# Nystrom attention with a sticky expert, one core: batch 0's queries and keys in single pairs, landmark sums on GpSimd, fewer first w1 transfers

## The chip, the core and the metric

The kernel runs on one core of a Trainium2 chip. Its engines work side by side and wait for each other through semaphores: TensorE (PE) multiplies into PSUM, VectorE (DVE) and ScalarE (ACT) work on PSUM and SBUF, GpSimd (POOL) on SBUF, and SyncE (SP) issues nearly all transfers (DMA). The metric is the device time of one execution in microseconds (us). Before the change the median of three runs is 450.06 us, from 449.97 to 450.13.

## The reference

Inputs are q, k and v of 8 batches with 8 heads, 576 tokens and 64 features, and the weights of 8 experts (w1 512 x 1024, w2 1024 x 512). First comes attention through 32 landmarks per head, each the mean of 18 neighbouring tokens:

```
q_lm = q.reshape(B, H, m, S // m, D).mean(axis=3)      # m = 32
k_lm = k.reshape(B, H, m, S // m, D).mean(axis=3)
A, Bm, C = sm(q, k_lm), sm(q_lm, k_lm), sm(q_lm, k)    # scaled softmax
Z = Bm.T / (norm1(Bm) * norminf(Bm) + 1e-06)
for _ in range(6):
    Z = 2 * Z - Z @ Bm @ Z
attn_out = A @ Z @ C @ v
```

Its output is the input of a mixture of experts: every token has the logits of 8 experts, takes the best one or keeps the expert of the token before it (by a local gate), and its output is `p[e] * (max(x @ w1[e], 0) @ w2[e])`.

## The kernel before

The batches go one after the other. Of each batch the attention part gives the factor `at` (A, transposed) and a small matrix `wt` (Z C v); x is never formed, since w1 is multiplied by `wt` into `g` (`w_w1`, L1236, for some 128-column blocks of w1 at a time, and `first_w1`, L1251, for block 0, whose slices of all 8 experts are loaded ahead). `split_g` (L1260) makes a high part `gh` on ScalarE and a low part `gl` on VectorE. `mm1` (L1286) then makes the hidden rows of block f out of six products (`gh` with two parts of `at`, and `gl` with one, for each of two head groups), and `expert` (L1313) the outputs with w2. One expert, chosen by a vote of the batch's tokens, serves a whole batch; the tokens of other experts are gathered at the end.

The order on each engine is the order in which this Python code emits instructions. Later batches' attention steps are spread between the expert's products by a table of times; `clock` and `at_time(t, ...)` put a step at a place and not at a time on the chip. Batch 0 has nothing to hide behind: `startup` (L933) is written out by hand. The names in it:

- `load` (L227) issues q and k of a batch. Heads lie in pairs (128 partitions hold two heads of 64 features), and a transfer moves one or two of four pairs. Every transfer has one of eight semaphores in turn, so a transfer waits until the one eight places before it has landed.
- `landmarks` (L254) sums 18 tokens to a landmark on VectorE, with GpSimd's help from batch 1 on; `landmark_scale` (L271) scales on ScalarE. For keys it writes the 32 landmarks behind the keys, so that a score product of 288 + 32 columns has those of the landmarks too.
- `score_c(g, hf, bank)` (L959) is C's scores of head group g, half hf of the tokens; `score_a` (L968) A's. `max_c`, `max_b`, `max_both` (L976 to L985) take maxima on VectorE, `max_b` with an exponential on ScalarE behind it; `exp_c` is C's exponentials; `turn_a` transposes A's scores.
- `lq0`, `lk0`, `lq2`, `lk2` are batch 1's landmarks in parts. `vote` (L859) leaves the expert's number in `regs`; SyncE and TensorE read it into a register, and the expert's weights are loaded (`load_w1` L1229, `load_w2` L1271).
- `keep_busy` (L926) and the loops at L189, L191 and L1174 are products whose result nobody reads.
- `second_block` (L1197) emits batch 1's scores C (`c_products`, L613), of which `c_max` (L624) takes maxima, together with blocks 1 to 3 of the first expert's w1.

Of the kernel before, what the change touches and what calls it, by code (L numbers as in the profile page):

```python
# [13 lines left out]
F32 = mybir.dt.float32  # L14
# [5 lines left out]
AX = mybir.AxisListType  # L20
# [4 lines left out]
P = 128  # L25
B, H, S, D = 8, 8, 576, 64
M = 32
# [36 lines left out]
def nystrom_attn_then_sticky_moe(ctx, tc, qT, kT, v, wg, w12, out):  # L64
# [121 lines left out]
        nc.vector.memset(ecs[g][:, S:], 0.0)  # L186
    nc.vector.memset(v_t[64:128, 4 * DM:], 0.0)
    pz = one.tile([P, 512])
    for _ in range(11):  # L189
        nc.tensor.matmul(pz, zeros[:, 0:P], zeros, start=True, stop=True)  # L190
    for _ in range(18):  # L191
        nc.tensor.matmul(pz[:, 0:16], zeros[:, 0:P], zeros[:, 0:16], start=True, stop=True)


    events, clock, serial = [], [0.0], itertools.count()
# [20 lines left out]
    def at_once(parts):  # L216
        for _ in parts:
            pass
# [8 lines left out]
    def load(b, st):  # L227
        for t in "qk":
            load_qk(b, st, t, b % 2)
        q, k = ("q", qT, S), ("k", kT, S)  # L230
        pieces = [(x, slice(a, a + 2)) for a in (0, 2) for x in (q, k)]
        if b == 0:
            pieces[2:] = [(x, slice(a, a + 1)) for x in (q, k) for a in (2, 3)]
        for (t, src, n), a in pieces:
            nc.sync.dma_start(out=st[t][:, a, 0:n], in_=src[b][:, a])
        if b == 0:
            nc.sync.dma_start(out=wg_sb[0:D], in_=wg)
# [16 lines left out]
    def landmarks(b, st, t, a):  # L254


        src = st[t][:, :, 0:S].rearrange("p a (l t) -> p a l t", t=SEG)
        s = sm.tile([P, 2, M], F32, name="s" + t)
        if b == 0:
            for i in (0, 1) if a else (slice(0, 2),):  # L260
                nc.vector.reduce_sum(out=s[:, i], in_=src[:, a + i] if a else src[:, i], axis=AX.X)  # L261
        else:
            t9 = at.tile([P, 2, M, 9], F32, name="t9")
            for i in range(2):
                nc.gpsimd.tensor_add(t9[:, i], src[:, a + i, :, 0:9], src[:, a + i, :, 9:18])  # L265
            yield 1
            nc.vector.reduce_sum(out=s, in_=t9, axis=AX.X)  # L267
            yield 0.75
        landmark_scale(st, t, a, s)

    def landmark_scale(st, t, a, s):  # L271
# [338 lines left out]
    def c_begin_rest(st, banks):  # L610
        st["pc"][1].extend(x.tile([P, 512])[:, 0:96] for x in banks)

    def c_products(st, k0, n):  # L613


        out, x = (st["pc"][1], 0) if k0 == 512 else (st["pc"][0], k0)
        for c in range(4):
            for g in range(2):
                h = head(g, c)
                r = slice(64 * (h % 2), 64 * (h % 2) + 64)  # L620
                nc.tensor.matmul(out[g][32 * c:32 * c + 32, x:x + n], st["ql"][r, h // 2, :],
                                 st["k"][r, h // 2, k0:k0 + n], start=True, stop=True)
# [310 lines left out]
    def startup(st, nx):  # L933
# [34 lines left out]
        def score_a(g, hf, bank):  # L968
            pa[g, hf] = bank[0].tile([P, 512], F32, name=bank[1])
            for c in range(4):  # L970
                h = head(g, c)
                r = slice(64 * (h % 2), 64 * (h % 2) + 64)
                nc.tensor.matmul(pa[g, hf][32 * c:32 * c + 32, 0:288], st["k"][r, h // 2, S:S + M],
                                 st["q"][r, h // 2, 288 * hf:288 * hf + 288], start=True, stop=True)

        def max_c(g, hf):  # L976
            nc.vector.reduce_max(out=nm[g][:, hf:hf + 1], in_=pc[g, hf][:, 0:288], axis=AX.X, negate=True)
# [14 lines left out]
        def turn_a(g, hf):  # L992
            nc.vector.transpose(out=sa[:, g, 9 * hf:9 * hf + 9, :].rearrange("p j l -> p (j l)"), in_=pa[g, hf][:, 0:288])

        at_once(landmarks(0, st, "q", 0))
        score_c(0, 0, (psa, "one"))
        at_once(landmarks(0, st, "k", 0))
        score_c(0, 1, (psa, "one"))
        score_a(0, 0, (py, "py"))
        score_a(0, 1, (pg, "pg"))  # L1000
        max_c(0, 0)
        at_once(landmarks(0, st, "q", 2))
        score_c(1, 0, (psa, "one"))
        at_once(landmarks(0, st, "k", 2))
        score_c(1, 1, (py, "py"))
        max_c(0, 1)
        max_b(0)
        max_both(0)
        turn_a(0, 0)
        max_b(1)  # L1010
        exp_c(0)
# [159 lines left out]
        vote(st, lq0)  # L1171
        keep_busy(3)
        pz = one.tile([P, 512])
        for _ in range(22):  # L1174
            nc.tensor.matmul(pz[:, 0:16], ones, ones[:, 0:16], start=True, stop=True)

        e = st["e"] = expert_of(regs[0:1, 0:1], (ET.SP, ET.PE))
        st["w1", 0] = load_w1(e, 0, ((nc.sync, 1, 1, 0, P), (nc.sync, 2, 1, 0, P), (nc.sync, 3, 1, 0, P)))
        get_w2(0, 0)
        get_w2(0, 1)  # L1180
        st["w1", 1] = load_w1(e, 1, ((nc.sync, 0, 2, 0, P), (nc.sync, 2, 2, 0, P)))
        get_w2(0, 2)
        get_w2(0, 3)
        mine = sm.tile([P, 1], F32, name="mine0", bufs=1)
# [12 lines left out]
        def second_block():  # L1197
            c_begin(nx, (one, one))
            c_begin_rest(nx, (one, Banks((pg, "pg"))))
            c_products(nx, 0, 512)  # L1200
            lk2(0)
            lk2(1)
            g1 = w_w1(st, 0, 1, 1, ((py, "py"), (py, "py")))
            next(g1)
            c_products(nx, 512, 96)
            c_max(nx, 1, (0,))
            at_once(g1)

        at_time(0.02, second_block)
        at_time(0.6, c_max, nx, 1, (1,))  # L1210
        at_time(1.005, lambda: at_once(w_w1(st, 0, 2, 2, ((py, "py"), (py, "py")))))
        at_time(1.3, c_max, nx, 0)
        at_time(1.31, c_exp_b, nx)
        at_time(1.52, c_bound, nx)
# [625 lines left out]
```

## Time and profile before

| | |
|---|---|
| median of 3 runs | 450.06 us (449.97 to 450.13) |
| profiled execution | 451.21 us, its span on the core 449.4 us |
| TensorE busy | 435.1 us (97%), 4898 products |
| VectorE busy | 284.5 us (63%) |
| ScalarE busy | 216.0 us (48%) |
| GpSimd busy | 192.0 us (43%) |
| chain that ended last | PE 77%, DVE 13%, ACT 5%, issue 2%, DMA 1%, POOL 1% |

Times in rows count from the span's start. Busy time is what instructions of an engine cover; the times of products are modelled ends of a pipelined engine. The chain is followed back from the last instruction, at each step to what released it. A share of the whole span says little about a stage: the first 41 us, which the change touches, have their own limits.

### The profile page before, as it was taken

To read this page: it belongs to the slowest core of one execution; us is meant where nothing else is said; L and a number is where in the kernel's file an instruction comes from. 1 tells how busy PE (TensorE), PEld (TensorE's weight loads), DVE (VectorE), ACT (ScalarE), POOL (GpSimd) and SP (SyncE) were. 2 spreads that over 40 slices of the span, in tenths; PEclk is the share of its full clock that TensorE was granted. 3 is DMA by queue.
4 is the path that set the end of the run, shared out by engine and by line. 5 is a ranking of instruction groups with operands and counts; after the bars stand their busy time and mean duration, and the time that the engine had idled before them with its cause. 6 is when DMAs were issued, how large, how long until landed. Compare 5 with 4: busy or idle time off the path is not lost.

```text
span 449.4 us, 12512 instructions
## 1 busy us (share of the span) xinstructions
PE 435.1 (97%) x4898; PEld 337.1 (75%) x4898; DVE 284.5 (63%) x869; ACT 216.0 (48%) x577; POOL 192.0 (43%) x235
## 2 busy tenths in 40 slices
PE   8888999999999999999999999999999999999996
PEld 3455777777786788878887788788887778776885
DVE  7878786666858576665766574656555786954111
ACT  2546525467354751566253752465145414445611
POOL 5456663165815664263632650174116601055520
PEclk9999999999999999999999999999999999999999
DMA  8959952779569697649957615831164315692211
GB/s 303 378 198 350 367 190 98 268 287 261 210 160 382 202 388 159 245 164 341 290 138 260 237 54 125 318 110 48 55 233 158 113 44 173 252 313 95 97 31 50
DMA packets 62365, 91.53 MB, mean 204 GB/s; under 512 B 26731, under 2 KB 28267, under 8 KB 61152
## 3 DMA queue, kind: packets, MB, share of 16 engines
q1 hardware_dynamic: 60960, 86.23, 57.0%
q0 software_dynamic: 1344, 4.48, 2.7%
q8 instruction: 39, 0.64, 0.6%
q14 instruction: 22, 0.18, 0.1%
HBM read 75.27 MB, written 15.47 MB: 202 GB/s over the span
## 4 chain that ended last, share of the span: by engine, by line
PE 77%; DVE 13%; ACT 5%; issue 2%; DMA 1%; POOL 1%; SPq 0%; DVEq 0%; ACTq 0%; POOLq 0%
PE py L1337 33%; PE ph L1295 19%; PE pg L1346 5%; PE ph L1247 2%; PE one L416 2%; PE one L463 1%; DVE h L1307 1%; PE one L562 1%; PE py L1573 1%; DMA k_t<-kT 1%; PE one L517 1%; DVE gl L1269 1%; PE one L825 1%; POOL t L265 1%; DVE sk L261 1%
## 5 line engine op out<-in xcount | busy, mean ns | idle before, releaser
L1337 PE MATMUL py<-wh,h 128*128 128x512 f32 x504 | 161.6, 403 | 0.1
L1284 POOL TENSOR_TENSOR wl<-raw,wh 128x512 fp32r<-128x512 f32 x64 | 82.2, 1293 | 70.8 <-ACT wh L1282 69.7
L1302 ACT ACTIVATE h<-ph 128x256 fp32r<-128x256 f32 (+1 forms) x128 | 52.4, 413 | 111.2 <-PE ph L1295 94.2
L1337 PEld LDWEIGHTS py<-wh,h 128*128 128x128 f32 x504 | 86.4, 189 | 25.2 <-issue 13.2
L1307 DVE SCALAR_TENSOR_TENSOR h<-ph,h 128x256 fp32r<-128x256 f32 x128 | 53.0, 416 | 61.0 <-ACT h L1302 58.2
L1337 PE MATMUL py<-wl,h 128*128 128x512 f32 x252 | 80.5, 400 | 0.0
L1295 PE MATMUL ph<-ath,gh 128*128 128x320 f32 (+1 forms) x256 | 77.5, 303 | 1.5 <-ACT gh L1266 0.8
L1295 PE MATMUL ph<-ath,gl 128*128 128x320 f32 (+1 forms) x256 | 75.8, 296 | 0.0
L1295 PE MATMUL ph<-atl,gh 128*128 128x320 f32 (+1 forms) x256 | 75.6, 295 | 0.0
L1295 PEld LDWEIGHTS ph<-ath,gh 128*128 128x128 f32 x256 | 48.4, 189 | 9.1 <-ACT h L1302 2.2
L1337 PEld LDWEIGHTS py<-wl,h 128*128 128x128 f32 x252 | 45.9, 188 | 11.6 <-issue 1.3
L1295 PEld LDWEIGHTS ph<-atl,gh 128*128 128x128 f32 x256 | 48.3, 189 | 3.9
L1295 PEld LDWEIGHTS ph<-ath,gl 128*128 128x128 f32 x256 | 48.3, 189 | 0.2 <-DVE gl L1269 0.2
L1282 ACT CAST wh<-raw 128x512 fp32r<-128x512 f32 x69 | 43.2, 627 | 2.2 <-DMA raw<-w 1.4
L1406 POOL TENSOR_TENSOR ys<-ys,yl 64x512 f32<-64x512 f32 x8 | 10.3, 1281 | 58.5 <-ACT yl L1404 58.5
L265 POOL TENSOR_TENSOR t<-q_t 128x288 f32<-128x288 f32 x20 | 14.5, 747 | 23.5 <-DVE sk L267 23.5
L423 DVE TENSOR_TENSOR et<-et,one 128x64 f32<-128x64 f32 x36 | 7.9, 220 | 24.7 <-ACT et L422 16.4
L794 POOL TENSOR_TENSOR sa<-sa,rsa 128x1152 f32<-128x1152 f32 x7 | 14.9, 2133 | 19.9 <-DVE s L693 13.2
L265 POOL TENSOR_TENSOR t<-k_t 128x288 f32<-128x288 f32 x22 | 17.0, 795 | 11.9 <-DVE sq L267 10.8
L1346 PE MATMUL pg<-wl,h 128*128 128x512 f32 x56 | 21.9, 391 | 0.0
L1346 PE MATMUL pg<-wh,h 128*128 128x512 f32 x56 | 21.8, 390 | 0.0
L1395 ACT ACTIVATE ys<-py,token 128x512 f32<-128x512 f32 x30 | 19.0, 685 | 5.0 <-PE py L1337 4.7
(435 smaller groups left out, 729.3 us busy)
## 6 DMA issues: line engine op xcount, KB each, us to landing
raw<-w SPq DMA_DIRECT2D x75, 256.0 KB
raw<-w SPq DMA_DIRECT2D x16, 1024.0 KB
k_t<-kT SPq DMA_DIRECT2D x9, 1152.0 KB
q_t<-qT SPq DMA_DIRECT2D x9, 1152.0 KB
out<-ys SPq DMA_DIRECT2D x31, 256.0 KB
v_t<-v SPq DMA_DIRECT2D x20, 256.0 KB
ad<-sa POOLq DMA_DIRECT2D x7, 576.0 KB, 3.1
v_t<-v SPq DMA_DIRECT2D x3, 1024.0 KB
```

Source lines behind the costliest of these rows:

```text
L265: nc.gpsimd.tensor_add(t9[:, i], src[:, a + i, :, 0:9], src[:, a + i, :, 9:18])
L416: return {1: lambda: each_place(lambda g, r: nc.tensor.matmul(pn[r, g, :], et[r, g, 0:32], et[r, g, n0:64], start=True, stop=True))}, part ...
L794: nc.gpsimd.tensor_tensor(out=sa, in0=sa, in1=rs.unsqueeze(2).broadcast_to([P, 2 * NJ, M]), op=ALU.mult)
L1282: by(out=wh, in_=raw)
L1284: rest.tensor_tensor(out=wl, in0=raw, in1=wh.bitcast(F32), op=ALU.subtract)
L1295: mm = nc.tensor.matmul(hp, w[:, g, c], x[:, g, s0:s0 + n], start=(i == 0), stop=(i == 5))
L1302: nc.scalar.activation(out=h[:, 0:e], in_=hp[:, 0:e], func=AF.Relu)
L1307: nc.vector.scalar_tensor_tensor(out=h[:, 384:384 + m], in0=hp[:, 0:m], scalar=0.0, in1=h[:, 0:m].bitcast(F32), op0=ALU.max, op1=ALU.subtract)
L1337: nc.tensor.matmul(yps[k], h[:, part + i * P:part + i * P + P], w, start=(f == 0 and part == 0 and w is wh), stop=(f == NC2 - 1 and part = ...
L1346: nc.tensor.matmul(yps[4], hs[ff][1], w, start=(ff == 0 and w is w2[ff][0]), stop=(ff == NC2 - 1 and w is w2[ff][1]))
L1395: nc.scalar.mul(out=ys, in_=yp, mul=st["pw"][:, k:k + 1])
L1406: nc.gpsimd.tensor_tensor(out=ys[0:64], in0=ys[0:64], in1=yl[0:64], op=ALU.add)
```

## The change

In `load`, batch 0's q and k go in eight transfers of one pair each, queries 0 and 1, keys 0 and 1, queries 2 and 3, keys 2 and 3, instead of six. In `startup`, the sums of these landmarks are taken apart: pairs 0 and 1 and queries 2 and keys 3 on VectorE alone, queries 3 and keys 2 first in GpSimd (18 tokens added to 9) and then on VectorE (`landmark_sums`). The maxima of group 0 move ahead of the last landmark sums. The first weights are issued as two transfers (block 1, blocks 2 and 3) and one (second half), instead of three and two. In `second_block` half of the large score products, two of four places of both groups, moves behind the product with w1 block 1, and the score products of the last 64 tokens and the landmarks move behind those with blocks 2 and 3. The warm-up products before the start are 12 wide ones instead of 11 wide and 18 small ones, and 39 small ones instead of 22 stand before the first product with w1.

```diff
-    for _ in range(11):
+    for _ in range(12):
         nc.tensor.matmul(pz, zeros[:, 0:P], zeros, start=True, stop=True)
-    for _ in range(18):
-        nc.tensor.matmul(pz[:, 0:16], zeros[:, 0:P], zeros[:, 0:16], start=True, stop=True)
...
         if b == 0:
-            pieces[2:] = [(x, slice(a, a + 1)) for x in (q, k) for a in (2, 3)]
+            pieces = [(x, slice(a + i, a + i + 1)) for a in (0, 2) for x in (q, k) for i in (0, 1)]
...
-    def c_products(st, k0, n):
+    def c_products(st, k0, n, places=range(4)):
...
-        for c in range(4):
+        for c in places:
...
-        at_once(landmarks(0, st, "q", 0))
+        (_, q01), (_, k01), (q23_half, q23), (k23_half, k23) = [landmark_sums(st, t, a) for a in (0, 2) for t in "qk"]
+        q23_half(1)
+        k23_half(0)
+        q01(0, True)
+        q01(1, True)
         score_c(0, 0, (psa, "one"))
-        at_once(landmarks(0, st, "k", 0))
+        k01(0, True)
+        k01(1, True)
         score_c(0, 1, (psa, "one"))
         score_a(0, 0, (py, "py"))
         score_a(0, 1, (pg, "pg"))
+        q23(0, True)
         max_c(0, 0)
-        at_once(landmarks(0, st, "q", 2))
+        max_b(0)
+        max_c(0, 1)
+        max_both(0)
+        q23(1)
         score_c(1, 0, (psa, "one"))
-        at_once(landmarks(0, st, "k", 2))
+        k23(0)
+        k23(1, True)
         score_c(1, 1, (py, "py"))
-        max_c(0, 1)
-        max_b(0)
-        max_both(0)
         turn_a(0, 0)
...
-        for _ in range(22):
+        for _ in range(39):
             nc.tensor.matmul(pz[:, 0:16], ones, ones[:, 0:16], start=True, stop=True)
 
         e = st["e"] = expert_of(regs[0:1, 0:1], (ET.SP, ET.PE))
-        st["w1", 0] = load_w1(e, 0, ((nc.sync, 1, 1, 0, P), (nc.sync, 2, 1, 0, P), (nc.sync, 3, 1, 0, P)))
+        st["w1", 0] = load_w1(e, 0, ((nc.sync, 1, 1, 0, P), (nc.sync, 2, 2, 0, P)))
         get_w2(0, 0)
         get_w2(0, 1)
-        st["w1", 1] = load_w1(e, 1, ((nc.sync, 0, 2, 0, P), (nc.sync, 2, 2, 0, P)))
+        st["w1", 1] = load_w1(e, 1)
...
-            c_products(nx, 0, 512)
+            c_products(nx, 0, 512, (0, 1))
             lk2(0)
             lk2(1)
             g1 = w_w1(st, 0, 1, 1, ((py, "py"), (py, "py")))
             next(g1)
-            c_products(nx, 512, 96)
+            c_products(nx, 0, 512, (2, 3))
             c_max(nx, 1, (0,))
             at_once(g1)
...
         at_time(1.005, lambda: at_once(w_w1(st, 0, 2, 2, ((py, "py"), (py, "py")))))
+        at_time(1.007, c_products, nx, 512, 96)
         at_time(1.3, c_max, nx, 0)
```

The function that GpSimd's halves come from stood there before, for batch 1: `half(i)` adds 9 tokens to 9 on GpSimd, `part(i, alone)` sums 18 of the source (alone) or 9 of GpSimd's result on VectorE, and part 1 is followed by the scaling.

VectorE's instructions in the start, before, from the first landmark sum on (`DMAHW0` to `DMAHW7` are the eight semaphores of the transfers; `one`, `py` are PSUM banks):

```order
L261 TENSOR_REDUCE sq<-q_t_217 128x64 [waits DMAHW0_49]
L261 TENSOR_REDUCE sk<-k_t_218 128x64 [waits DMAHW1_49]
L977 TENSOR_REDUCE nm<-one 128x1 [waits PE_49]
L261 TENSOR_REDUCE sq<-q_t_217 128x32 [waits DMAHW2_49]
L261 TENSOR_REDUCE sq<-q_t_217 128x32 [waits DMAHW3_49]
L261 TENSOR_REDUCE sk<-k_t_218 128x32 [waits DMAHW4_49]
L261 TENSOR_REDUCE sk<-k_t_218 128x32 [waits DMAHW5_49]
L977 TENSOR_REDUCE nm<-one 128x1 [waits PE_49]
L980 TENSOR_REDUCE nm<-one 128x1
L985 TENSOR_TENSOR nm<-nm 128x1 [waits DVE_49]
L993 STREAM_TRANSPOSE sa<-py 128x288 [waits PE_49]
L980 TENSOR_REDUCE nm<-py 128x1 [waits PE_49]
```

The same engine and place after the change, from queries 2 on, behind the four single sums of pairs 0 and 1 (`h` holds GpSimd's halves; L971, L974, L979, L987 are the old L977, L980, L985, L993):

```order
L307 TENSOR_REDUCE sq<-q_t_200 128x32 [waits DMAHW4_49]
L971 TENSOR_REDUCE nm<-one 128x1 [waits PE_49]
L974 TENSOR_REDUCE nm<-one 128x1 [waits PE_49]
L971 TENSOR_REDUCE nm<-one 128x1 [waits Activation_49]
L979 TENSOR_TENSOR nm<-nm 128x1 [waits DVE_49]
L307 TENSOR_REDUCE sq<-h 128x32 [waits Pool_49]
L307 TENSOR_REDUCE sk<-h 128x32 [waits Pool_49]
L307 TENSOR_REDUCE sk<-k_t_201 128x32 [waits DMAHW7_49]
L987 STREAM_TRANSPOSE sa<-py 128x288 [waits PE_49]
L974 TENSOR_REDUCE nm<-py 128x1 [waits PE_49]
```

Two maxima and the minimum of group 0 now stand ahead of the last three landmark sums; the second of the wide maxima has a wait for ScalarE, and two sums wait for GpSimd.

GpSimd's instructions at this place after the change; before, the rows without L304 stood there alone:

```order
L113 IOTA t_94 128x64 [waits Pool_49]
L304 TENSOR_TENSOR h<-q_t_200 128x288 [waits DMAHW5_49]
L115 CAST eb<-t_94 128x128 [waits Pool_49]
L304 TENSOR_TENSOR h<-k_t_201 128x288 [waits DMAHW6_49]
L101 IOTA t_94 128x8 [waits Pool_49]
L103 CAST ranks<-t_94 128x8 [waits Pool_49]
```

The halves stand between constants, and a constant behind a half waits with it for the landing.

VectorE in the second block, before, from the low parts of w1 block 0 on:

```order
L1269 TENSOR_TENSOR gl<-py,gh 128x128 [waits Activation_49] x2
L313 TENSOR_REDUCE sk<-h 128x32 [waits Pool_49] x2
L631 TENSOR_REDUCE nm8c<-one 128x1 [waits PE_49]
L1269 TENSOR_TENSOR gl<-py,gh 128x128 [waits Activation_49] x2
L1307 SCALAR_TENSOR_TENSOR h<-ph,h 128x256
L1310 SCALAR_TENSOR_TENSOR atl<-ph,atl 128x64
L631 TENSOR_REDUCE nm8c<-one 128x1
```

TensorE in the second block, after, behind the products of hidden block 0 (L615 is `c_products`, the old L621; L1249 the product with w1, the old L1247; L1297 `mm1`, the old L1295):

```order
L615 MATMUL one<-k_t_214,ql 32x512 x4
L1249 MATMUL py<-raw_630,wt 32x128 x8
L615 MATMUL one<-k_t_214,ql 32x512 x4
L1297 MATMUL ph<-ath,gh 128x320
L1297 MATMUL ph<-atl,gh 128x320
L1297 MATMUL ph<-ath,gl 128x320
```

Before, all eight of the first row stood ahead of the product with w1, and the small score products behind it. VectorE's order is as before here, but its first maximum reads what the second part of the score products writes.

## Rows read from the trace of the kernel before

**Rows 1.** Stages: engine busy us (instructions), then PEclk, DMA share, GB/s.
```profile
6.00:12.00 6.00, 5.11 (x75) 1.86 (x73) 5.80 (x12) 1.39 (x7) 1.56 (x8) 1.00 1.05 371
12.00:28.30 16.30, 13.43 (x293) 7.25 (x290) 13.43 (x46) 8.91 (x28) 8.77 (x9) 1.00 0.86 316
28.30:41.00 12.70, 10.65 (x141) 6.84 (x138) 9.86 (x34) 6.64 (x30) 7.41 (x10) 1.00 0.83 269
41.00:449.40 408.40, 401.15 (x4390) 319.40 (x4386) 252.26 (x769) 197.42 (x511) 169.26 (x165) 1.00 0.58 194
```
**Rows 2.** Chain that ended last, first 14 us: start, length, what.
```profile
1.20 4.75 DMA k_t<-kT
...
10.84 0.79 PE py L965 x8
...
11.65 0.20 DVE nm L980
```
**Rows 3.** VectorE in order of time: start, us, engine, line, op, operands.
```profile
5.97 1.35 DVE L261 TENSOR_REDUCE sk<-k_t 128x64 f32<-128x1152 f32 x1
...
7.62 1.40 DVE L261 TENSOR_REDUCE sq<-q_t 128x32 f32<-128x576 f32 x2
8.99 1.50 DVE L261 TENSOR_REDUCE sk<-k_t 128x32 f32<-128x576 f32 x2
10.41 0.45 DVE L977 TENSOR_REDUCE nm<-one 128x1 f32<-128x288 f32 x1
...
12.29 0.17 DVE L176 TENSOR_SCALAR sums<-sums 128x2 f32<-128x2 f32 x1
```
**Rows 4.** SyncE's issues in order of time.
```profile
5.97 0.38 SPq L235 DMA_DIRECT2D q_t<-qT  x1
7.47 0.38 SPq L235 DMA_DIRECT2D k_t<-kT  x1
...
9.74 0.47 SPq L941 DMA_DIRECT2D wg_sb<-wg  x1
```
**Rows 5.** ScalarE behind the group 1 maximum.
```profile
11.88 0.29 ACT L981 ACTIVATE bm<-py,nm 128x32 f32<-128x32 f32 x1 [0.44 <-DVE nm L980]
```
**Rows 6.** A half on GpSimd, and the sum of one on VectorE, batch 1's.
```profile
20.99 0.74 POOL L310 TENSOR_TENSOR h<-q_t 128x288 f32<-128x288 f32 x1
...
23.74 0.41 DVE L313 TENSOR_REDUCE sk<-h 128x32 f32<-128x288 f32 x1
```
**Rows 7.** TensorE, its weight loads and VectorE in the second block.
```profile
28.38 0.70 PE L1175 MATMUL one<-ones 128*128 128x16 bf16 x22
31.46 1.09 PE L621 MATMUL one<-k_t,ql 64*32 64x512 f32 x16
32.39 0.18 PEld L1247 LDWEIGHTS py<-raw,wt 64*32 64x32 f32 x16 [0.75 <-DMA raw<-w]
32.39 0.45 PE L1247 MATMUL py<-raw,wt 64*32 64x128 f32 x16
32.64 0.69 DVE L631 TENSOR_REDUCE nm8c<-one 128x1 f32<-128x512 f32 x1 [0.86 <-PE one L621]
33.25 0.48 DVE L1269 TENSOR_TENSOR gl<-py,gh 128x128 fp32r<-128x128 f32 x2
```
**Rows 8.** GpSimd, VectorE and TensorE around TensorE's gap at 39 us.
```profile
36.89 0.61 POOL L1282 CAST wh<-raw 128x512 fp32r<-128x512 f32 x1 [0.49 <-DMA raw<-w]
37.58 1.29 POOL L1284 TENSOR_TENSOR wl<-raw,wh 128x512 fp32r<-128x512 f32 x1
37.59 1.34 DVE L849 SCALAR_TENSOR_TENSOR eq<-pe,keys 128x40 f32<-128x40 f32 x1
39.94 0.59 PE L1247 MATMUL ph<-raw,wt 64*32 64x512 f32 x1 [0.97 <-DVE atl L1310]
```
**Rows 9.** Wide products whose result nobody reads, early and late.
```profile
1.23 4.88 PE L190 MATMUL one<-sa 128*128 128x512 bf16 x11 [1.23 <-DVE sa L180]
...
26.59 1.04 PE L930 MATMUL one<-ones 128*128 128x512 bf16 x4
```

More of the change, by code (lines that the diff above doesn't have):

```diff
@@ L258, in landmarks @@
         s = sm.tile([P, 2, M], F32, name="s" + t)
[L259 to L268, printed above, removed]
+        t9 = at.tile([P, 2, M, 9], F32, name="t9")
+        for i in range(2):
+            nc.gpsimd.tensor_add(t9[:, i], src[:, a + i, :, 0:9], src[:, a + i, :, 9:18])
+        yield 1
+        nc.vector.reduce_sum(out=s, in_=t9, axis=AX.X)
+        yield 0.75
         landmark_scale(st, t, a, s)
```

## The prediction

> **What bounds the kernel now.** I read the busy times by stage first, then the chain of waits of the first 14 us, then VectorE, SyncE, ScalarE and GpSimd in order of time there, and last the stretch from 28 to 41 us. From 41 us to the end TensorE is busy 401.15 of 408.40 us [rows 1]: nothing that the change touches lies there, and a shift of what comes before is carried to the end one for one. From 6 to 12 us VectorE is the busy one, 5.80 of 6.00 us [rows 1]. The chain of that stretch [rows 2] goes from the landing of batch 0's first key pairs (1.20 + 4.75 = 5.95) through VectorE to the last score product on TensorE at 10.84 and a maximum on VectorE at 11.65. I take this last point, the group 1 maximum, as the measure of the start: from there on both kernels issue the same VectorE, ScalarE and TensorE instructions down to the vote, in the same order, each waiting for the one before. So whatever moves 11.65 moves the vote, the expert's first loads and the end.
>
> **The start, step by step.** Before, VectorE runs without a gap from 5.97 to 10.49: keys 0 and 1 (1.35), a maximum, queries 2 and 3 (1.40), keys 2 and 3 (1.50) [rows 3]. What is left (a maximum of 0.45 at 10.41, a small one, a minimum, a transpose) is done while ScalarE and TensorE turn the last landmarks into scores, from 10.49 to 11.65: 1.16 us of cover. The new order spends this cover earlier: only the transpose stays behind the last landmark sum, the rest goes ahead of it.
>
> When do the pairs land? SyncE shows it: its later transfers wait for a landing each, of keys 0 and 1 at 5.97, queries 2 at 7.47, keys 3 at 9.74 [rows 4]. The three pairs behind queries 2 take 2.27, some 0.75 each, which puts queries 3 at 8.23 and keys 2 at 8.98. The bytes ahead of key pair 1 stay the same, so I leave its landing at 5.97. Splitting gains this: pair 0 is summed before pair 1 lands, and after 5.97 one sum of half of 1.50 = 0.75 remains instead of 1.35: done at 6.72 instead of 7.32, 0.60 gained.
>
> From 6.72 VectorE does: queries 2, 0.70 (half of 1.40), to 7.42; the first maximum, 0.45, to 7.87; the group 0 maximum, whose scores are ready at 6.72 + 1.16 = 7.88, 0.20, to 8.08. Then the next maximum waits for ScalarE, by the order. In the trace the same pair of steps stands at 11.65: the maximum of 0.20 [rows 2] ends at 11.85, ScalarE's exponential starts at 11.88 [rows 5], and VectorE goes on behind it at 12.29 [rows 3]: 0.44 of standstill. So 8.52; a maximum of 0.45 and the minimum to 9.07; two sums of GpSimd's halves at 0.41 [rows 6], to 9.87; keys 3 alone, 0.75, to 10.6; and the 1.16 of ScalarE and TensorE behind it: 11.75. So 0.60 from the split and 0.58 from GpSimd's halves (two times 0.70 less 0.41) are eaten by the wait of 0.44 and by the maxima and the minimum, some 0.8, that lost their cover: **+0.1 us**.
>
> That is with landings by size. The trace has one that is not: 5.97 to 7.47 is 1.50 for one pair, twice 0.75, and all later ones keep that delay [rows 4]. Before, it cost nothing, VectorE was busy. After, queries 2 are wanted at 6.72. If they land at 7.47 again, VectorE stands 0.75; GpSimd starts queries 3 at 8.23 and, with 0.74 a half [rows 6] and a small cast that the order puts between its two halves, ends keys 2 at about 9.9; VectorE ends keys 3 at 11.35: 12.5, or **+0.85**. GpSimd is strictly in line: what waits behind its first half is that cast, the second half and two constants that are needed much later. As the trace is one execution and doesn't show the delay's cause, I take the middle of the ends, **+0.5**; the lower bound is -0.35, if the wait for ScalarE were hidden.
>
> [...]
>
> The warm-up ends with its twelfth wide product; the next product but one waits for ScalarE anyway: nothing. SyncE's eight issues are ahead of the data: nothing.
>
> **28 to 41 us.** (a) 39 instead of 22 small products: 22 take 0.70 [rows 7], so 17 more are at most 0.54, by the spacing rather 0.43, and the large scores, behind expert 0's first products, move from 31.46 to about 31.9. Half of them (of 1.09) ends at 32.45, and the first w1 slice is waited for until 32.39 [rows 7]: hidden, and if the slice lands earlier nothing is gained. (b) In the new order the other half, 0.55, stands behind that w1 product of 0.45, and VectorE's maximum over all of them ahead of the low halves "gl". Before, that maximum began at 32.64 and gl at 33.25 [rows 7]. Now the scores end at 33.4, the maximum (0.69) at 34.1, gl follows: 0.75 to 0.85 later, and TensorE's third product of that slice waits for it. So TensorE is late by 0.7. (c) Two w1 transfers and one for the second half, instead of three and two: each saves SyncE some 0.5, but the transfer engines are 83% busy in this stretch [rows 1]; the landing gains 0 to 0.35.
>
> Against this stands the gap of TensorE before 39.94, 0.97 us [rows 8]. What ends it is VectorE: the step at 37.59 lasts 1.34 while GpSimd's subtraction runs from 37.58 for 1.29 [rows 8]; the products free their bank only after that. A delay of 0.7 puts this step at about 38.3, still inside GpSimd's subtraction, whose cast waits for a weight landing and not for TensorE (0.49 before 36.89 [rows 8]). So the gap takes up the delay: 0, with bounds -0.35 (loads earlier) and +0.3 (if (a) and (b) add up beyond 0.97). I take **-0.05**.
>
> **Sum.** +0.5 - 0.05 = +0.45 on the profiled execution's 451.21 us (span 449.4, 1.8 around it); it is 1.15 above the median of the timed runs, and the same difference on 450.06 gives **450.5 us**. What a measurement of this kernel can tell from no change is about 0.2%, 0.9 us: 449.16 to 450.96.
>
> **Rivals.**
> 1. The loads come forward (faster). If splitting lets key pair 1 land one pair earlier (0.75), and the fewer w1 transfers free VectorE's step at 37.59 and the second half's product, it is -0.65 in the start and -0.35 to -0.9 later: about 449.0. For it: 4.75 us from issue to landing [rows 2], where four pairs at 0.75 need 3.0. Against it: the bytes ahead of key pair 1 are unchanged.
> 2. The landings decide (slower). Place: VectorE's wait for queries 2 and GpSimd's waits for queries 3 and keys 2. Where the delay of 0.75 returns and a second one falls on queries 3 or keys 2, nothing of it is covered any more; price 0.85 + 0.75 = 1.6: 451.6. It decides once keys 2 land after about 8.7 (0.74 later GpSimd ends when VectorE is ready, 9.07 + 0.41). For it: there is such a delay, in the one execution traced [rows 4]. Against: the three pairs behind it keep 0.75.
> [...]
> 4. GpSimd's halves save nothing, since VectorE waits for them: the upper end of the forecast, +0.85, 450.9.
>
> **Chances.** The forecast with its own range, 449.9 to 451.0: 0.55. Rival 1: 0.19. Rival 2: 0.16. Rival 3: 0.05. Rival 4 by itself: 0.05. The whole range, 449.0 to 451.4, leaves out rival 3 and the far ends of 1 and 2. Faster than 449.16: most of rival 1, 0.16. Slower than 450.96: rivals 2 and 3 and a small part of the forecast, 0.24. Within: 0.60.
>
> **What would show it.** The group 1 maximum between 11.6 and 12.5; VectorE idle for about 0.4 behind the group 0 maximum, waiting for ScalarE; key pair 1's landing at 5.9 to 6.0; VectorE waiting for queries 2 if SyncE's second batch 1 transfer starts at 7.4, and not if at 6.7; gl of the second w1 slice 0.7 later against the start of that slice, and the gap before the second half's w1 product smaller by as much. The prediction is wrong if that maximum comes before 11.2, if the ScalarE wait is missing, if the gap at 39 us stays beside the delayed gl, or if the granted clock falls.

## The result, and the profile after

The changed kernel takes 453.31 us (median of 5 runs, 452.73 to 455.02), the kernel before 450.06 (449.97 to 450.4): a ratio of 1.0079, 95% interval 1.0062 to 1.0095. It is slower by 3.25 us where 450.5 was forecast, outside the range of 449.0 to 451.4. The profiled execution took 454.88 us, its span 453.1. Executions of over 800 us, which a few kernels had, are left out of every ratio.

The first thing to see is in the page's slices, TensorE's busy tenths and its granted clock: a dent in the first two slices, and a lower clock in the third, which the kernel before does not have. Before, then after:

```profile
PE   8888999999999999999999999999999999999996
PEclk9999999999999999999999999999999999999999
```

```profile
PE   7689999999999999999999999999999999999996
PEclk9989999999999999999999999999999999999999
```

Then by stages (engine busy us, then PEclk, DMA share, GB/s), against the second row of [rows 1], where the clock is 1.00 from 12 to 28.3 us:

```profile
20.00:22.00 2.00, 1.14 (x50) 0.78 (x49) 1.94 (x6) 0.48 (x1) 2.00 (x3) 1.00 1.04 382
22.00:24.00 2.00, 0.92 (x30) 0.74 (x33) 0.51 (x3) 0.68 (x1) 2.00 (x3) 0.67 1.04 382
24.00:26.00 2.00, 2.00 (x43) 1.09 (x42) 1.55 (x5) 0.52 (x2) 0.10 (x2) 0.50 0.40 144
26.00:28.00 2.00, 1.79 (x23) 0.64 (x21) 1.10 (x3) 0.68 (x3) 1.77 (x2) 0.97 0.00 0
```

TensorE in order of time there (start, us, engine, line, op, operands; in brackets the idle time ahead and what ended it):

```profile
20.73 0.41 PE L667 MATMUL pg<-v_t,ect 128*32 128x64 f32 x10
23.09 0.86 PE L667 MATMUL pg<-v_t,ect 128*32 128x64 f32 x22 [1.95 <-issue]
...
25.05 1.32 PE L924 MATMUL ph<-ones 128*128 128x512 bf16 x3
```

In the middle of 32 equal products TensorE stands for 1.95 us and waits for nothing that the profile shows ("issue"). Behind it the granted clock is 0.50 until about 26: a wide product takes 0.44 (3 in 1.32) as in the warm-up of [rows 9], not 0.26. The chain that ended last holds this standstill as a piece of its own:

```profile
21.14 1.95 issue
25.11 1.26 PE ph L924 x3
```

The start was late too. VectorE, against [rows 3]:

```profile
6.10 1.64 DVE L307 TENSOR_REDUCE sk<-k_t 128x32 f32<-128x576 f32 x2 [0.89 <-DMA k_t<-kT]
7.83 0.75 DVE L307 TENSOR_REDUCE sq<-q_t 128x32 f32<-128x576 f32 x1
...
9.53 0.46 DVE L971 TENSOR_REDUCE nm<-one 128x1 f32<-128x288 f32 x1 [0.45 <-ACT bm L975]
...
10.96 0.74 DVE L307 TENSOR_REDUCE sk<-k_t 128x32 f32<-128x576 f32 x1
...
12.86 0.19 DVE L974 TENSOR_REDUCE nm<-py 128x1 f32<-128x32 f32 x1 [0.77 <-PE py L959]
```

The group 1 maximum is at 12.86 instead of 11.65. SyncE's issues show why, as in [rows 4] (each waits for a landing: 6.98 for key pair 1, 7.82 for queries 2, 9.37 for keys 2, 10.15 for keys 3):

```profile
6.98 0.36 SPq L233 DMA_DIRECT2D q_t<-qT  x1
7.82 0.38 SPq L233 DMA_DIRECT2D k_t<-kT  x1
...
9.37 0.38 SPq L233 DMA_DIRECT2D k_t<-kT  x1
10.15 0.47 SPq L935 DMA_DIRECT2D wg_sb<-wg  x1
```

Key pair 1 lands at 6.96, not at the 5.97 that I had kept.

The way of the lateness through the traces, from the starts of equal instructions in both: +1.21 at the group 1 maximum, +4.04 at expert 0's first product (33.35 instead of 29.31), +3.58 at the second half of its w1 (43.52 instead of 39.94), +4.0 behind 132 us, +5.0 behind 212, +3.65 at the last product. The drop at the end is an accident of the trace of before: there TensorE's products over the last expert's w1 took 1.3 longer, from 408.31 on, with a wait at 409.59. Of the other traces only the four at the end of the experiments (r1 to r4) have it, and by its size it makes up the difference between the 451.21 of that execution and the median of 450.06.

### The profile page after: what moved, and what is told of

Its sections match the earlier page's. It is cut to its first block, busy times and chain, and to the rows that moved or that the text cites. A ratio compares the mean times of both kernels' runs of the same rounds, so it can differ in the third digit from the quotient of the medians.

```text
span 453.1 us, 12512 instructions
## 1 busy us (share of the span) xinstructions
PE 436.3 (96%) x4898; PEld 338.0 (75%) x4898; DVE 283.6 (63%) x871; ACT 215.9 (48%) x577; POOL 193.3 (43%) x237
## 4 chain that ended last, share of the span: by engine, by line
PE 78%; DVE 12%; ACT 5%; issue 2%; DMA 1%; POOL 1%; SPq 0%; DVEq 0%; ACTq 0%; POOLq 0%
PE py L1339 33%; PE ph L1297 19%; PE pg L1348 5%; PE ph L1249 2%; PE one L410 2%; PE one L457 1%; PE one L556 1%; DVE h L1309 1%; PE py L1575 1%; DMA q_t<-qT 1%; PE one L511 1%; PE one L819 1%; POOL t L259 1%; PE ph L1554 1%; DVE gl L1271 1%
## 5 line engine op out<-in xcount | busy, mean ns | idle before, releaser
L1297 PE MATMUL ph<-ath,gh 128*128 128x320 f32 (+1 forms) x256 | 77.5, 303 | 1.1 <-ACT gh L1268 0.4
L1297 PE MATMUL ph<-ath,gl 128*128 128x320 f32 (+1 forms) x256 | 75.9, 296 | 0.4 <-DVE gl L1271 0.4
L1297 PE MATMUL ph<-atl,gh 128*128 128x320 f32 (+1 forms) x256 | 75.6, 295 | 0.0
L1297 PEld LDWEIGHTS ph<-ath,gh 128*128 128x128 f32 x256 | 48.4, 189 | 9.2 <-ACT h L1304 2.2
L1339 PEld LDWEIGHTS py<-wl,h 128*128 128x128 f32 x252 | 45.9, 188 | 11.6 <-issue 1.3
L1297 PEld LDWEIGHTS ph<-atl,gh 128*128 128x128 f32 x256 | 48.3, 189 | 3.9
L1297 PEld LDWEIGHTS ph<-ath,gl 128*128 128x128 f32 x256 | 48.3, 189 | 0.9 <-DVE gl L1271 0.8
L788 POOL TENSOR_TENSOR sa<-sa,rsa 128x1152 f32<-128x1152 f32 x7 | 15.0, 2137 | 20.7 <-DVE s L687 14.0
```

What stands on the lines that cost most here:

```text
L788: nc.gpsimd.tensor_tensor(out=sa, in0=sa, in1=rs.unsqueeze(2).broadcast_to([P, 2 * NJ, M]), op=ALU.mult)
L1297: mm = nc.tensor.matmul(hp, w[:, g, c], x[:, g, s0:s0 + n], start=(i == 0), stop=(i == 5))
L1339: nc.tensor.matmul(yps[k], h[:, part + i * P:part + i * P + P], w, start=(f == 0 and part == 0 and w is wh), stop=(f == NC2 - 1 and part = ...
```

## The experiments

The kernel before, run beside the others each time, had medians of 450.47 (e1 to e4), 450.23 (e5, e7 to e9), 450.50 (e10, e11) and 450.13 (e12, e13). A ratio is not the quotient of two medians and can differ from it by some 0.2%.

**Two theories.** Theory F: TensorE's instructions come in blocks, by transfers of their own. The traces of before and after hold 9921 of them: 4898 products, as many weight loads, and 125 that its sequencer runs (waits, registers). Counted all together, in order of time, four are places at which TensorE stands, in one trace or in several, without a releaser and goes on 1.2 to 1.5 us behind the end of a packet of one kind: the 450th, the 706th, the 3522nd and the 5570th, which are 256, 12 times 256 and 20 times 256 behind the first. (Without those of the sequencer the distances are not multiples of 256.) The packets are instructions, 39 of 16 KB on a queue of their own (the page; queue and kind: packets, MB, share), and 39 times 256 is 9984, about TensorE's 9921:

```profile
q8 instruction: 39, 0.64, 0.6%
```

Among the transfers of 20.5 to 20.6 us is the one that matters (packets, MB, share of that tenth of a microsecond):

```profile
q8 instruction: 1, 0.02, 68.5%
```

It takes 1.10 us from 20.53, and TensorE goes on 1.46 behind its end. I call the block from the 450th instruction on block 3, the one from the 706th block 4. In before, block 3's fetch begins at 15.49 and is ready 1.3 ahead of its need, if TensorE can go on 1.46 behind its end there too. The warm-up lost 18 small products and gained a wide one; with their weight loads that is 34 instructions less, so the edge behind which block 3 is asked for by this theory (the 194th) moved from 13.3 to 16.7 us. Theory L: the late landings, and what follows from them, are the whole cause.

**1. The pairs back (e1).** The changed kernel, with before's warm-up and small products.

```diff
-    for _ in range(12):
+    for _ in range(11):
         nc.tensor.matmul(pz, zeros[:, 0:P], zeros, ...)
+    for _ in range(18):
+        nc.tensor.matmul(pz[:, 0:16], zeros[:, 0:P], zeros[:, 0:16], ...)
...
-        for _ in range(39):
+        for _ in range(22):
```

> The changed kernel with the warm-up of before (11 wide and 18 small products) and 22 instead of 39 small products behind the vote. Theory F (instruction fetch): TensorE's instructions come in blocks of 256, and block 3 (from the 450th traced instruction on) arrived at 23.09 us because the 34 instructions that were removed ahead of it made its request come some 3 us later; the standstill of 1.95 us and the half clock of 22.9 to 26 us follow from that. With the instructions back, no gap over 0.3 us at the 450th instruction, granted clock 1.00 throughout, and what is left is the start's shift of 0.5 to 1.25: 450.3 to 451.3 us. Rival L (landings): the late landings of batch 0's pairs and what follows from them are the cause; the standstill stays and the time too: 452.7 to 453.5.

Measured: 451.19 us, 1.0021 (1.0009 to 1.0033). The same products run through, and the only wait left is one for VectorE that before has as well; TensorE:

```profile
20.22 0.65 PE L669 MATMUL pg<-v_t,ect 128*32 128x64 f32 x32
21.38 0.33 PE L1058 MATMUL ph<-yl 32*32 32x32 f32 x16 [0.51 <-DVE yl L1065]
```

**2. The pairs away, nothing else (e2).** The same edit the other way round, on the kernel before.

> The kernel before with the changed warm-up alone (12 wide products, no small ones) and 39 small products behind the vote; all else as before. F: the request of block 3 moves from 13.3 to about 15.5 us, the block is ready at 20.2 to 21.9 and wanted at 19.6: a gap of 0.6 to 2.3 us at the 450th instruction, and perhaps a lower clock behind it; 450.6 to 452.5 us. L: 449.9 to 450.3, no gap.

Measured: 451.96 us, 1.0039 (1.0024 to 1.0055), single times from 450.66 to 455.9, granted clocks from 1.00 down to 0.990. Its trace has the standstill, at the 450th instruction; TensorE:

```profile
19.98 0.41 PE L671 MATMUL pg<-v_t,ect 128*32 128x64 f32 x10
22.46 0.86 PE L671 MATMUL pg<-v_t,ect 128*32 128x64 f32 x22 [2.07 <-issue]
```

These two decide for F. About half of the loss, by e1 rather seven tenths, is made by a part of the change that computes nothing.

**3. The start alone (e3), the second block alone (e4).** e3 is e1 with the w1 transfers and large scores of before; e4 is the kernel before with those two changed.

```diff
-        st["w1", 0] = load_w1(e, 0, ((nc.sync, 1, 1, 0, P), (nc.sync, 2, 1, 0, P), (nc.sync, 3, 1, 0, P)))
+        st["w1", 0] = load_w1(e, 0, ((nc.sync, 1, 1, 0, P), (nc.sync, 2, 2, 0, P)))
...
-            c_products(nx, 0, 512)
+            c_products(nx, 0, 512, (0, 1))
...
-            c_products(nx, 512, 96)
+            c_products(nx, 0, 512, (2, 3))
...
```

> The kernel before with the start alone changed: batch 0's q and k in single pairs, the halves on GpSimd and the new order; warm-up, small products, w1 transfers and the second block's scores as before. F: no gap at the 450th instruction; the group 1 maximum at 12.1 to 12.9 instead of 11.65, and the end later by as much: 450.3 to 451.3. L: 452.0 to 453.5. If the landing of key pair 1 at 6.96 was an accident of the one traced execution, it lands at 5.9 to 6.2 here and the maximum comes at 11.7 to 12.1: 450.0 to 450.5.

> The kernel before with the other part alone: fewer w1 transfers and the large scores in two halves by place; start, warm-up and small products as before. F and the prediction: the low halves of the second w1 slice about 0.7 later, taken up by the gap at 39 us: 449.7 to 450.4. Rival: this part costs what is not explained by the fetch: 451.0 to 452.5.

Measured: e3 451.43, 1.0018 (1.0009 to 1.0027), no standstill at the 450th, key pair 1 at 7.11 and the maximum at 12.90. e4 450.50, 1.0004 (0.9993 to 1.0014). So the start costs about 0.8 us (0.18% of 450), the second block nothing that the interval shows, and the moved pairs the rest: 0.58% as what e1 leaves of 0.79, 0.39% when measured alone.

**4. The single pairs alone (e7).** All sums and their order as before.

```diff
         if b == 0:
-            pieces[2:] = [(x, slice(a, a + 1)) for x in (q, k) for a in (2, 3)]
+            pieces = [(x, slice(a + i, a + i + 1)) for a in (0, 2) for x in (q, k) for i in (0, 1)]
```

> The kernel before with batch 0's transfers in eight single pairs, all sums and their order as before. Theory S (splitting itself delays): key pair 1 lands at 6.5 to 7.1 instead of 5.95, since the third of the smaller transfers comes late on some of its engines and all behind it keep that; keys 3 at 9.5 to 10.2 and the group 1 maximum at 12.0 to 12.7 instead of 11.65. Rival A (an accident of single executions): key pair 1 at 5.9 to 6.1, maximum at 11.6 to 11.9. My prediction stood on A's landing, 5.97.

Measured (one execution, 450.45): key pair 1 at 6.84; SyncE's issue that waits for it, and VectorE's sum of keys 0 and 1, 0.96 later than in [rows 3]:

```profile
6.86 0.37 SPq L235 DMA_DIRECT2D q_t<-qT  x1
```

```profile
6.93 1.35 DVE L261 TENSOR_REDUCE sk<-k_t 128x64 f32<-128x1152 f32 x1 [1.09 <-DMA k_t<-kT]
...
12.45 0.19 DVE L980 TENSOR_REDUCE nm<-py 128x1 f32<-128x32 f32 x1 [0.20 <-PE py L965]
```

No accident: in all ten traces with single pairs key pair 1 lands at 6.4 to 7.4. The landings of the 16 engines show the pattern. In these ten the third transfer's last engine lands 0.65 to 1.57 behind the middle one, where the two transfers ahead of it have 0.11 to 0.36, and what is behind it keeps much of that. With whole pairs it is 0.72 to 1.33 in five traces, and 0.33 at most, as ahead of it, in two (e4, e13). In before the third is queries 2 (middle 6.54, last 7.45); in the changed kernel it is key pair 0 (middle 4.96, last 6.07).

**5. Moving the edges of the blocks (e5, e9, e8, e13).** In before itself a standstill of this kind sits ahead of the 706th instruction, in the products on which the vote waits; TensorE:

```profile
25.04 0.47 PE L825 MATMUL pg<-at,wgc 128*32 128x160 f32 x5
25.96 0.52 PE L825 MATMUL pg<-at,wgc 128*32 128x128 f32 x10 [0.46 <-issue]
```

e5, e9 and e13 are before with 8, 8 and 13 small products in the warm-up and 32, 40 and 27 behind the vote; e8 is the changed kernel with 11 wide and 3 small, and 37.

```diff
-    for _ in range(18):
+    for _ in range(8):
...
-        for _ in range(22):
+        for _ in range(32):
```

> The kernel before with 8 instead of 18 small products in the warm-up and 32 instead of 22 behind the vote, nothing else. In before's trace the fourth block (from the 706th traced instruction) was ready at 25.96, and TensorE stood 0.46 us for it in the middle of the products ahead of the vote; its request (19.3) waited for batch 1's loads until 23.2. Theory F (fetch): the blocks now end 20 instructions later in the program; block 3's request moves from 13.3 to about 13.6 and stays ahead of its need, and the edge of block 4 falls behind the products of the vote, among the keep-busy products: no gap at 25.5, vote 0.4 to 0.5 earlier, 449.4 to 450.1 us where before has 450.4. Rival: the standstills are not the fetch's or the landing decides: no change, 450.2 to 450.7.

> As the kernel with 8 and 32 small products, but 40 behind the vote, so that all later blocks end 16 instructions earlier in the program than before. F: the gap at 25.5 is gone as there; at the blocks' later ends the shortest time between two ends is 6.0 instead of 5.1 us by before's trace, so the standstills of 0.3 us (near 128 us) and 0.8 us (near 208 us), which five of six traces so far show one or both of, go too: 449.0 to 449.9 us. The 8 more small products may put the first expert product off by 0.2. Rival: later standstills stay or move to other blocks: as the kernel with 32.

> The changed kernel with 11 wide and 3 small products in the warm-up and 37 small ones behind the vote: a dose between the changed kernel (12 and 0) and the one with all pairs back (11 and 18). F: block 3's request comes at about 15.4 instead of 16.7 (changed) and 14.0 (all back); the standstill at the 450th instruction is between 0 and 1.2 us, not 1.95. Rival L (landings): standstill as in the changed kernel, 1.8 to 2.2.

> The kernel before with 13 small products in the warm-up and 27 behind the vote: half the step of the kernel with 8 and 32, whose block 3 was ready only 0.2 us ahead of its need in the profiled execution and, by its times of 449.5 to 455.3, too late in most. F: block 3 is ready 0.5 to 1.3 us ahead, block 4 late by 0.2 to 0.5; few or no executions above 451.5, median 449.9 to 450.6 where before has 450.3. Rival: times spread up to 455 as with 8; then any move of the edges towards a later place brings the standstill.

Measured: e5 452.81, 1.0051 (1.0028 to 1.0075); e9 452.42, 1.0043 (1.0022 to 1.0064); e13 453.22, 1.0050 (1.0027 to 1.0073); e8 453.99 in one execution, standstill 2.15 where at most 1.2 was expected. The hope for a faster kernel missed, and e9's trace keeps a standstill of 0.67 at 208 us that was to go. In e5's trace the 0.46 is gone, as expected:

```profile
24.91 0.98 PE L825 MATMUL pg<-at,wgc 128*32 128x160 f32 x16
```

But block 3 was ready only 0.2 ahead of its need there, and its twelve times fall in two groups: three from 449.5 to 450.1, nine from 451.3 to 455.3. e13, half the step, has four up to 450.57 and eight from 452.87, and its trace shows the standstill; TensorE:

```profile
19.12 0.42 PE L1055 MATMUL ph<-yl 32*32 32x64 f32 x15
21.78 0.31 PE L1055 MATMUL ph<-yl 32*32 32x64 f32 x1 [2.24 <-issue]
```

That the slower times of e5 and e9 are those with the standstill is not shown, since their only traces are of faster ones. I had the edges right and the margin wrong: I took the time from edge to fetch as 2 to 4 us, and it is 6.0 in e13.

**6. Smaller pieces ahead of the fetch (e10, e11).**

```diff
-        nc.sync.dma_start(out=firsts, in_=w12[:, 0, :, 0:512].rearrange("e p x -> p e x"))
+        for i in range(0, E, 2):
+            nc.sync.dma_start(out=firsts[:, i:i + 2], in_=w12[i:i + 2, 0, :, 0:512].rearrange("e p x -> p e x"))
```

e10 is the kernel before with this edit, e11 the changed kernel with it and with batch 1's q and k in single pairs.

> The kernel before with its 2 MB load of the first w1 slices (w1f) as four transfers of 512 KB, nothing else. In before, block 4 of TensorE's instructions was requested at 19.3 and its fetch began at 23.2, three microseconds into that load. Theory Q (the fetch is served when a transfer ahead of it on its engine ends): with shorter transfers it begins at 20.3 to 21.8, the standstill of 0.46 us at 25.96 is gone, the vote 0.3 to 0.5 earlier: 449.5 to 450.1 us where before has 450.2. Rival B (it waits for the whole backlog, whatever its pieces): it begins at 22.9 to 23.5, standstill and time as before.

> The changed kernel with batch 1's q and k in single pairs too and w1f in four transfers, so that what stands ahead of block 3's fetch (begun 3.8 us after the edge before it, at 20.53) is in smaller pieces. Q: the fetch begins 1 to 2.5 us behind the edge, and the standstill at the 450th instruction is 0 to 1.0 us instead of 1.95. B: it begins 3.5 to 5 us behind the edge, standstill 1.7 to 2.2.

Measured: e10 450.88, 1.0011 (0.9994 to 1.0028), no gain; its only trace is of an execution of 824 us and is compared with none here. e11 457.4 in one execution: the fetch begins 3.75 behind the edge, standstill 1.91, as with whole pairs. (Its time holds a second wait, 2.03 ahead of 44.79, with the clock at 0.50 behind it until 49.0.) Theory Q falls, B holds in e11.

**7. The same count at another place (e12).** The changed kernel with 17 small products in TensorE's wait at 9.8 us.

```diff
         q23(1)
+        gap = ph.tile([P, 512], F32, name="ph")
+        for _ in range(17):
+            nc.tensor.matmul(gap[:, 0:16], ones, ones[:, 0:16], ...)
         score_c(1, 0, (psa, "one"))
...
-        for _ in range(39):
+        for _ in range(22):
```

> The changed kernel, its warm-up as it is (12 wide products), with 17 small products put into TensorE's wait of 1.23 us behind the first score products (9.8 to 11.0) and 22 instead of 39 behind the vote. The same number of instructions stands ahead of the 450th as in the kernel before, but nothing is done for them in the warm-up. F (the edges of the instruction blocks): no standstill at the 450th instruction, group 1 maximum 12.3 to 13.0 as in the changed kernel, 450.7 to 451.6 us. Rival W (the small products of the warm-up themselves matter, for the clock or the first scores): the standstill stays, 452.7 to 455.

Measured: 453.34, 1.0091 (1.0063 to 1.0120). The trace is F's (a gap of 0.04 at the 450th instruction), the time is not: it lies in W's range. The fetch began at 17.54, 1.65 later than in e1, with the edge at the same 14.0, and block 3 came just as it was wanted; three of the six times, with clocks of 0.990 to 0.995, are 453.9 to 456.4 and leave room for executions in which it came too late, though none of these was traced; the three with clocks of 0.999 and 1.00 are 452.4 to 452.8. What the traced one of these lost is elsewhere, at 40 us: by the order of times the products wait for VectorE's last step on atl. GpSimd, VectorE and TensorE:

```profile
40.46 1.26 POOL L1289 TENSOR_TENSOR wl<-raw,wh 128x512 fp32r<-128x512 f32 x1
```

```profile
40.53 1.21 DVE L849 TENSOR_TENSOR wide<-fr,am 128x5 f32<-128x5 f32 x1
41.66 0.41 DVE L1312 SCALAR_TENSOR_TENSOR h<-ph,h 128x256 fp32r<-128x256 f32 x1
42.00 0.21 DVE L1315 SCALAR_TENSOR_TENSOR atl<-ph,atl 128x64 fp32r<-128x64 f32 x1
```

```profile
42.31 0.59 PE L1252 MATMUL ph<-raw,wt 64*32 64x512 f32 x1 [1.75 <-issue]
```

It is the meeting of [rows 8] again, VectorE's small step of 1.21 (0.17 in r4, the same kernel, and at 39.36 in e1) ends with GpSimd's subtraction, 41.74 beside 41.72; here the wait behind it is 1.75 instead of 0.97. What ties the two the rows do not show. In r4 no subtraction runs at that time, as in e1 (none from 38.60 to 42.32), and the wait is not there, so this loss is of single executions. Why the others of e12's times are slow is open.

**8. Four kernels once more (r1 to r4).** Is the place of the fetch drawn anew in each execution? The changed kernel, e1, e13 and e12 once more, unchanged.

> The changed kernel once more, for a second look at its own trace. If a program's fetch comes at its own place each time (theory P): begins at 20.0 to 21.0, standstill 1.7 to 2.3 at the 450th instruction. If it is drawn anew in each execution (theory D): it may begin at 17 to 19 and the standstill be under 1.

> The changed kernel with its pairs back in the warm-up, once more. P: the fetch begins at 15.3 to 16.5 as in all six traces with the edges where they are in before; no standstill; D: it may begin at 16.7 or later.

> The kernel before with 13 and 27 small products, once more; its first trace has the fetch at 19.26 and a standstill of 2.24, while 4 of its 12 times were at most 450.6. P: the fetch begins at 19.0 to 19.6 again. D: two times in three as before, else at 15.3 to 17 with no standstill and a time of about 450.5.

> The changed kernel with the 17 pairs in TensorE's wait, once more; its first trace has the fetch at 17.54, ready as the 450th instruction was wanted. P: 17.3 to 17.8 again, no standstill over 0.3, 452 to 453. D: 15.5 to 16.5 without a standstill, or 19 to 20.5 with one of 1.5 to 2.5 us.

Measured: 454.50, 453.70, 453.27 and 453.16, each with the last expert's late wait of before's trace; the kernel before took 451.17 beside them, once. From the edge to the fetch it is 3.86 us (first trace 3.82), 1.66 (1.88), 6.11 (5.98) and 3.50 (3.51): theory P for these traces. The changed kernel's TensorE, second trace, and the stage behind the standstill:

```profile
22.75 0.54 PE L667 MATMUL pg<-v_t,ect 128*32 128x64 f32 x22 [1.96 <-issue]
```

```profile
22.00:24.00 2.00, 1.25 (x63) 1.02 (x63) 0.58 (x3) 0.58 (x1) 1.68 (x2) 1.00 0.99 356
```

The standstill is the same, but the clock stayed at 1.00: the fall belongs to some executions, three of the seven traces with this standstill (the changed kernel's first, e2, e13). It cost 1.3 us in the changed kernel: from the standstill's end to expert 0's first product it is 10.26 with the fall and 9.00 without. In e2's times, five with a clock of 1.00 are 451.7 to 452.0, three with 0.990 to 0.996 are 453.7 to 455.9 (a fourth with 0.996 is 452.47, and one with 0.998 is 450.66).

All traces but e10's on one view (us; two executions where two were traced):

| kernel | block 3's fetch begins | TensorE is through block 2 | standstill |
|---|---|---|---|
| before, e4 | 15.49, 15.33 | 19.3, 19.5 | none |
| e1 | 15.89, 16.35 | 20.0, 20.7 | none |
| e3, e7 | 16.37, 16.17 | 20.5, 20.1 | none |
| e5, e9 | 16.74, 16.88 | 19.4, 19.5 | none |
| e12 | 17.54, 18.28 | 20.0, 20.7 | 0.04, 0.04 |
| e13 | 19.26, 19.61 | 19.5, 19.8 | 2.24, 2.28 |
| e2 | 19.97 | 20.4 | 2.07 |
| changed | 20.53, 20.23 | 21.1, 20.8 | 1.95, 1.96 |
| e8, e11 | 20.79, 20.78 | 21.2, 21.5 | 2.15, 1.91 |

By these rows TensorE stands if the fetch begins less than about 2.5 us (1.1 of transfer and 1.4 behind it) ahead of its need. Of the kernels tried none beats the one before.

## Why the prediction was wrong

**The failed step: "The warm-up ends with its twelfth wide product; ... nothing."** I priced the 17 products that left the warm-up by the work behind which they lay, and by that they were free. They were also 34 places in TensorE's instruction stream. Taken away alone (e2) they cost 1.8 us (0.39% of 450; 1.1 to 2.5 by the interval), given back (e1) they return about 2.6 (0.79% less 0.21%). The hint lay in a row that I left out: before's own 0.46 at 25.96 with "issue" as its releaser. The packets (39 of 16 KB) and the distances (256, and 12 and 20 times 256) agree with a program that comes in blocks. TensorE stood 1.91 to 2.28 us ahead of block 3 in seven of the seventeen traces; ahead of its fetch the DMA share is 1.04 to 1.05 (before and the changed kernel), and the 256 instructions up to it last 6.0 us in before (13.3 to 19.3) and 4.4 in the changed kernel (16.7 to 21.1).

**"I leave its landing at 5.97."** Wrong by 1.0, which put the group 1 maximum beyond the 11.6 to 12.5 that I gave: the delay that I had seen [rows 4] I hung on queries 2, and in fifteen of the seventeen traces it is the third transfer's, whose last engine lands 0.65 to 1.57 behind the middle one. The split made key pair 0 the third. What stands behind that landing held. My chain gave the maximum at landing + 5.78 (11.75 less 5.97): 12.74 for the changed kernel (measured 12.86), 12.34 for e1 (12.36), 12.89 for e3 (12.90), and within 0.26 in all nine traces with the new order. The start's 0.8 us in e3 lies inside my ends for it, -0.35 and +0.85; it is not this landing that put the time outside the range. The wait for ScalarE is there, 0.45 for the 0.44 forecast. VectorE starts on queries 2 0.03 behind their landing.

**"Whatever moves 11.65 moves the vote, the expert's first loads and the end."** Not one for one, even without the standstill. Where block 4 comes late, as in before, it and not the start sets the vote: e1's +0.71 at the maximum is +0.21 at the end of the products ahead of the vote, e7's +0.80 is +0.60.

**28 to 41 us: right on the whole, with bounds too narrow.** The 39 small products take 1.12 instead of 0.70, +0.42 where 0.43 was forecast by their spacing. The low halves of the second w1 slice are late, and the gap ahead of the second half's products is gone; TensorE in the changed kernel, against [rows 7] and [rows 8]:

```profile
31.94 1.12 PE L1176 MATMUL one<-ones 128*128 128x16 bf16 x39
33.35 1.13 PE L1259 MATMUL py<-w1f,ys 128*128 x8 [0.29 <-issue]
...
38.21 0.42 PE L1297 MATMUL ph<-ath,gl 128*128 128x320 f32 x1 [0.41 <-DVE gl L1271]
...
43.52 0.61 PE L1249 MATMUL ph<-raw,wt 64*32 64x512 f32 x1
```

The lateness falls from 4.04 to 3.58 over this stretch, and e4 puts the whole part at 1.0004. The delay is taken up as I said: in [rows 8] a VectorE step that begins inside GpSimd's subtraction ends with it (38.93 beside 38.87), and in the changed kernel a step that begins 1.05 into the subtraction, 0.30 long where e1 has 0.19, does too, at 42.27 beside 42.20:

```profile
40.92 1.28 POOL L1286 TENSOR_TENSOR wl<-raw,wh 128x512 fp32r<-128x512 f32 x1
```

```profile
41.97 0.30 DVE L841 TENSOR_TENSOR pe<-lg,mxl 128x40 f32<-128x40 f32 x1
```

The gap is no accident: all eight traces with the second block of before have it (0.81 to 1.07, and 1.37 behind a weight's landing in e2). With the new second block it is gone, or 0.14, in five of nine, and in the other four it is 0.49 (r2), 0.58 (e8), 1.75 (e12) and 2.03 (e11), and the stretch is 0.4 to 2.0 longer than in before, past the +0.3 that I allowed: in e12 a VectorE step close ahead of the last one on atl lasts 1.21 instead of 0.17 and ends with a subtraction (41.74 beside 41.72).

**The rivals.** Rival 3, with a chance of 0.05, was a lower granted clock. From 6 to 14 us the clock is 1.00 in all seventeen traces. It fell to 0.50 behind the standstill at 21 us, at a cost of 1.3 us, and the time is lost without it too (r1, 454.50). Rival 2's price, 1.6 in the start, was 1.2, by another landing than the three it named. Rival 1 had nothing to show. Rival 4's wait is not there: VectorE takes GpSimd's halves at 10.24 and 10.60 without idle time, and they were done at 9.37 and 10.30.

**Later standstills.** Two more of the kind, 0.3 near 132 us and 0.8 near 212, add to the changed kernel's trace what before's does not have; TensorE:

```profile
212.50 0.20 PE L443 MATMUL one<-wg_sb,wt 64*32 64x9 f32 x2 [0.80 <-issue]
```

The 17 products more behind the vote keep these edges at the instructions where they were, and one or both standstills are in thirteen of the sixteen other traces, e1 and e4 among them, so they hang neither on the moved pairs nor on the new start. Of one kernel one execution has them and another has not (0.67 near 209 us in r4, none in e12), and the only trace of before has none. How often before has them in its timed executions, and so whether they make a part of the 3.25, is open.

## What to carry to other kernels

Look for idle rows of TensorE with no releaser and count the instructions between them, with those that its sequencer runs; if they are 256 apart, a "free" filler instruction is a place in the program: here 34 instructions less moved a block edge from 13.3 to 16.7 us. Not every such row is one of these: the 0.29 ahead of 33.35 and the 1.75 of e12 stand elsewhere. Before trusting the first sums of a kernel, look at which transfer in order comes late, not at which tensor: in fifteen of the seventeen traces here the lateness is the third transfer's, in whole pairs and in single ones. And price a chain's start only up to the next thing that comes by itself, here an instruction block.

## What the runs showed that was not expected

The time from the block edge to its fetch went with the program and not with the count alone: 1.7 to 2.2 us in before, e1, e3, e4 and e7, 3.3 to 3.5 in e5, e9 and e12, 3.8 to 6.1 in e2, e8, e11, e13 and the changed kernel, and the two traces of one kernel agree within 0.25. Some late fetches begin as batch 1's last transfers land (20.53 beside 20.38 to 20.57 in the changed kernel's first trace), others do not (20.23 beside 19.38 to 19.57 in its second). Why a program gets an early or a late place was not found: the pieces' size does not decide it (e11), nor the count of instructions (e12), and e5's and e13's groups of times suggest that an execution can still fall to the other side. Also open is why the third transfer has stragglers.
